# One product moved from GpSimd to VectorE, and narrowing steps spread one to a place, in a linear-attention and expert kernel

## The chip, the cores and the metric

The kernel runs on one core of one Trainium2 chip. The metric is the device time of one execution in microseconds; the value shown is the median of several runs of the same program. One more execution was taken by the hardware profiler, and every duration below comes from it.

## The reference, cut to what matters

Three parts follow one another: a gated linear recurrence over 768 time steps for 4 batches of 8 heads of width 48, a routing of the 3072 resulting tokens to 8 experts of 384 places each, and a feed-forward layer on all tokens. The change touches only the time in which the first part runs.

```python
def _attn_ref(q, k, v, f_logit):
    B, H, S, D = q.shape                      # 4, 8, 768, 48
    f = 1.0 / (1.0 + np.exp(-f_logit))
    state = np.zeros((B, H, D, D), dtype=np.float32)
    for t in range(S):
        state = f[:, :, t, :, None] * state + np.einsum('bhd,bhe->bhde', k[:, :, t], v[:, :, t])
        y[:, :, t] = np.einsum('bhd,bhde->bhe', q[:, :, t], state)
...
h = np.maximum(x[mask] @ w1[e], 0.0); out[mask] = h @ w2[e]      # expert e, its 384 tokens
...
h = x @ w_in; g = h * np.clip(h + 3.0, 0.0, 6.0) / 6.0; return (g @ w_out).astype(np.float32)
```

The weights `moe2_w_in` and `moe2_w_out` (and the experts' weights) reach the kernel as 64-bit floats; q, k, v and the decay logits are 32-bit.

## The kernel before, in words

**Units and chunks.** The recurrence is computed in chunks of 128 time steps (`C`), 24 of them (`NCH`). Two chunks make a unit of 256 steps, of which there are 12 (`NU`). Batch and time are laid end to end, so a batch is three units, and every sixth chunk starts with an empty state. Two neighbouring time steps lie in one row of 96 numbers, so a 128-row tile holds a unit, and the even step of each pair is first folded into the odd one.

**Preparing a unit.** The logits, q and k of unit u are loaded into tiles `fr`, `qr` and `kr`. `decay` (L74) makes the decay `ft` on ScalarE in two steps (L76, L77), and on VectorE the product of a pair's two decays into `pmf` (L78). `keys` (L79) writes `pmk`: on VectorE the even key times the odd step's decay (L81), on ScalarE a copy of the odd key (L82). `queries` (L83) writes `pmq` in the same way: the even query times its decay (L85), which is the product that the change moves, and a copy (L86). TensorE then transposes these tiles (L91, L112) into PSUM tiles `pT`, ScalarE copies the decays out (L94), VectorE runs running products forward (L98) and backward (L106) and scales the transposed queries and keys by them into `qt` and `kh` (L125).

**Eight slots.** That preparation of unit u is cut into slots 0 to 7 (`slot`, L129; the tables `PET` and `OPS` say which TensorE and VectorE work a slot has). While chunk j is computed, `attention` walks four of them: slots 0 to 3 while `ti` is 0, slots 4 to 7 while `ti` is 1. `tg(i)` (L277) writes one slot. In a chunk the order of the code is: slot 0 or 4; the output of the chunk before (`l_mm`, L223: TensorE L227, ScalarE copy L232, VectorE logits L229); slot 1 or 5; the scores (`ya_mm`, TensorE L145 and L151), their copy out of PSUM on ScalarE (L177) and masking on GpSimd (L178); the values (`y_mm`, TensorE L202, ScalarE copy L203); the state's products (`kv_mm`, L213), whose VectorE addition (L220, or L218 on a batch's first chunk) and GpSimd scaling (L221) wait in the list `late` for the next slot; slot 2 or 6; the decays and, for `ti` 1, the queries of the unit after; the transposed keys (`kt_mm`, L185, L186); slot 3 or 7; and for `ti` 1 the keys of the unit after.

**Narrowing.** In the same time a generator `prep` turns 64-bit weights into pairs of 32-bit numbers. For each of 12 blocks of `moe2_w_in` (`prep_in`, L928, tiles `pw` for the two words and `pm` for the result) there are three steps: A, the split of the block before (ScalarE L720 rounds `pm` into `wih`, GpSimd L721 subtracts it from `pm` into `wil`) and VectorE's shift L923; B, VectorE's L925; C, VectorE's L927 and the load of the block two further on (L933, two buffers). After them come 8 blocks of `moe2_w_out` in four steps each (`prep_out`, L947: L958 on ScalarE with L923; L963 on VectorE; L925; L927). `take` (L275) draws steps at each slot, by a table, and a second table draws some at a chunk's end:

```python
PREP=((2,0,1,0),(0,0,2,0)); END=(0,1)
...
for _ in range(PREP[ti][i] if j<20 else 2): next(prep,None)
...
if j<20:
    for _ in range(END[ti] if j>=0 else 0): next(prep,None)
```

Both tables give three steps to a chunk, so a unit carries two blocks of `moe2_w_in`. From chunk 20 on every slot takes two. A slot runs its first VectorE operation, then the steps, or the additions in `late` first where the slot has no operation of its own.

**Order.** Every engine and the SyncE queue, which issues all these loads and stores, execute in the order in which the code writes them; nothing is rearranged. After the last chunk the routing for the first expert follows, then the loading of that expert's weights and tokens, then eight experts' matrix products, which fill TensorE to the end.

Of the kernel before, what the change touches and what calls it, by code (L numbers as in the profile page):

```python
# [17 lines left out]
def attention(tc, q,k,v,f,wg, x_dram, lg, ident, pmin, ranges, prep, setup, spin):  # L18
    nc=tc.nc
    ctx=ExitStack()  # L20
    with ctx:
# [11 lines left out]
        ft=cs.tile([128,2,H,D],F32,name="ft")  # L33
# [27 lines left out]
        def load(u,nm,h0=0,h1=H):  # L61
            b,o=divmod(u*U,S)
            if nm!='v':
                src={'f':f,'k':k,'q':q}[nm]
                t=ld.tile([128,H,2*D],F32,name=nm+"r",bufs=1) if h0==0 else raw[nm,u]
                nc.sync.dma_start(t[:,h0:h1],bass.AP(tensor=src.tensor,offset=src.offset+b*H*S*D+h0*S*D+o*D,ap=[[2*D,128],[S*D,h1-h0],[1,2*D]]))
            else:
                t=VP[u%2]
                for c in range(2):
                    nc.sync.dma_start(t[:,c,:,:D],bass.AP(tensor=v.tensor,offset=v.offset+b*H*S*D+(o+c*C)*D,ap=[[D,C],[S*D,H],[1,D]]))  # L70
            raw[nm,u]=t
        view=lambda u,nm: raw[nm,u].rearrange("p h (r d) -> p r h d",d=D)
        home=lambda nm,r: perm[nm][:,r].rearrange("p a s d -> p (a s) d")[:,:,:48]
# [8 lines left out]
            else: nc.scalar.copy(home('k',1)[:,h0:h1],x[:,1])  # L82
        def queries(u,i,h0=0,h1=H):  # L83
            x=view(u,'q')[:,:,h0:h1]
            if i==0: nc.gpsimd.tensor_tensor(out=home('q',0)[:,h0:h1],in0=x[:,0],in1=ft[:,0,h0:h1],op=OP.mult)  # L85
            else: nc.scalar.copy(home('q',1)[:,h0:h1],x[:,1])  # L86
        KH={};QT={};PC={};PX={};SX={}
        V=nc.vector
# [12 lines left out]
        def kept(u):  # L101
            PC[u]=pmin[:,u]
            nc.scalar.copy(PC[u],PX[u][:,:,:,G])
# [25 lines left out]
        def slot(u,n,fill=None):  # L129

            if u<NU and n in PET: PET[n](u)
            for f,*a in OPS.get(n,()) if u<NU else ():
                f(u,*a)
                if fill: fill(); fill=None
            while late: late.pop(0)()
            if fill: fill()
# [16 lines left out]
        def ya_mm(j):  # L153

            S=s_mm(j) if 0<=j<NCH and j%6 else None
            A=a_mm(j+1) if j+1<NCH else None
            if not S or not A:
                for p in range(NP):
                    for h in range(2):
                        for s in range(2):  # L160
                            if A: A(p,s,h)
                if S:
                    for p in range(NP):
                        for s in range(2): S(p,s)
                return
            for i,p in enumerate((0,2,1,3,None,None)):
                for s in range(2):
                    if p is not None: S(p,s)
                for s in range(2):
                    if i<2 or i>3: A(i if i<2 else i-2,s,1-s)  # L170
                for s in range(2):
                    if i>1: A(i-2,s,s)
        def a_ev(j,s):
            if s==0:
                AM[j]=wk.tile([128,2,NP,C],F32,name="am")
            am=AM[j][:,s]
            nc.scalar.copy(am,pA[j][s])  # L177
            nc.gpsimd.affine_select(out=am,in_=am,pattern=[[0,NP],[1,C]],compare_op=OP.is_ge,fill=0.0,base=0,channel_multiplier=-1)  # L178
        def kt_mm(j):
            u,c=divmod(j,2)  # L180
            if j%6==5: return
            kt=wk.tile([128,4,2,64],F32,name="kt")
            pk=ps.tile([128,NP,128],F32,name="pT",bufs=PB)
            for p in range(NP):
                nc.tensor.transpose(pk[:,p],KH[u][:,p,c*C:(c+1)*C],ident)  # L185
            nc.scalar.copy(kt.rearrange("p a s d -> p a (s d)"),pk)  # L186
            KT[j]=kt
        YT={};PY={}
        def y_mm(j,part):

            u,c=divmod(j,2); first=j%6==0
            vr=raw['v',u]; last=j==NCH-1
            rows=[slice(64*s,64*s+64) for s in range(2)]
            if part==0:
                if last: PY[j]=[ps.tile([128,NP,C],F32,name=f"pA{i}") for i in range(2)]
                else: PY[j]=[ps.tile([128,NP,C],F32,name="pT",bufs=PB) for _ in range(1 if first else 2)]*(2 if first else 1)
                return
            yt=wk.tile([128,NP,C],F32,name="yt")
            for p in (0,2,1,3):
                py=PY[j][p%2]  # L200
                for s in range(2):
                    nc.tensor.matmul(py[rows[s^p%2],p],vr[:,c,2*p+s],AM[j][:,s,p],start=first,stop=first or p>1)  # L202
                if p>1 and not first: nc.scalar.copy(yt[:,p%2::2],py[:,p%2::2])  # L203
            if first: nc.scalar.copy(yt,py)
            YT[j]=yt
        def kv_mm(j):
            u,c=divmod(j,2); first=j%6==0
            if j%6==5 or j>=NCH: return
            vr=raw['v',u]
            pk=ps.tile([128,512],F32,name="pT",bufs=PB)[:,:NP*D].rearrange("p (a d) -> p a d",a=NP)  # L210
            for p in range(NP):
                for s in range(2):
                    nc.tensor.matmul(pk[64*s:64*s+64,p],KT[j][:,p,s],vr[:,c,2*p+s,:D],start=True,stop=True)  # L213
            sn=St[(j+1)%2][:,:,:D]; so=St[j%2][:,:,:D]
            def update():
                pcb=PC[u][:,:,c][:,:,None].to_broadcast([128,NP,D])
                if first:
                    nc.vector.tensor_tensor(out=sn,in0=pk,in1=pcb,op=OP.mult)  # L218
                else:
                    nc.vector.tensor_add(so,so,pk)  # L220
                    nc.gpsimd.tensor_tensor(out=sn,in0=so,in1=pcb,op=OP.mult)  # L221
            late.append(update)
        def l_mm(j):  # L223
            W=2*D+8
            px=ps.tile([128,512],F32,name="pT",bufs=PB)[:,:NP*W].rearrange("p (a e) -> p a e",a=NP)
            for p in (0,2,1,3):
                nc.tensor.matmul(px[:,p],YT[j][:,p],SW[:,p],start=True,stop=True)  # L227
            y=wk.tile([128,NP,2*D],F32,name="y")
            def logits(): nc.vector.tensor_reduce(lg[:,j],px[:,:,2*D:].rearrange("p a e -> p e a"),axis=AX.X,op=OP.add)  # L229
            if j==NCH-1: logits()  # L230
            else: late.append(logits)
            nc.scalar.copy(y,px[:,:,:2*D])  # L232
            later.append(lambda: nc.sync.dma_start(x_dram[j*C:(j+1)*C,:],y.rearrange("p a d -> p (a d)")))
# [26 lines left out]
        def refill(u,nm,i):  # L260
            if u<NU:
                {'f':decay,'k':keys,'q':queries}[nm](u,i)
                if u+1<NU and i==(0 if nm=='f' else 1): later.append(lambda: load(u+1,nm))
# [3 lines left out]
        next(prep)  # L267
        while later: later.pop(0)()
        constants,early=setup()
        PREP=((2,0,1,0),(0,0,2,0)); END=(0,1)  # L270
        for j in range(-1,NCH+1):
            tu,ti=divmod(j+1,2)
            tu+=1
            if j>=0 and j%2==0 and j//2+1<NU: load(j//2+1,'v')
            def take(i):  # L275
                for _ in range(PREP[ti][i] if j<20 else 2): next(prep,None)
            def tg(i): slot(tu,4*ti+i,(lambda: take(i)) if j>=0 else None)  # L277
            if j==NCH: spin(lambda: ps.tile([128,384],F32,name="pT",bufs=PB),TAIL[0])
            tg(0)
            if 0<=j-1<NCH: l_mm(j-1)  # L280
            if j==NCH: spin(lambda: ps.tile([128,384],F32,name="pT",bufs=PB),TAIL[1])
            tg(1)
            while later: later.pop(0)()
            if 0<=j<NCH: y_mm(j,0)
            ya_mm(j)
            if j+1<NCH:
                a_ev(j+1,0)
                a_ev(j+1,1)
            if ti==1: refill(tu+1,'f',2)
            if 0<=j<NCH: y_mm(j,1)  # L290
            if j>=0: kv_mm(j)
            tg(2)
            if ti==0 and tu<NU: kept(tu)
            if ti==0: refill(tu+1,'f',0)
            if j+1<NCH: kt_mm(j+1)
            if ti==1:
                for i in range(2): refill(tu+1,'q',i)
            tg(3)
            if ti==0: refill(tu+1,'f',1)
            if ti==1:  # L300
                for i in range(2): refill(tu+1,'k',i)
            if j>=0: next(constants,None)
            if j>=NCH-4: next(ranges,None)
            if j in (17,22,24): next(early)
            if j<20:
                for _ in range(END[ti] if j>=0 else 0): next(prep,None)
# [55 lines left out]
class Routing:  # L362
# [67 lines left out]
    def spin(s,tile,n):  # L430

        if not n: return
        t=tile()
        for _ in range(n): s.tc.nc.tensor.matmul(t[:,:128],s.ones,s.before,start=True,stop=True)
# [715 lines left out]
```

## Time and profile before

| | us |
|---|---|
| median of 3 runs (839.98 to 841.34) | 841.13 |
| the profiled execution's own time | 845.23 |
| its span, first to last instruction | 843.2 |
| TensorE busy in the span (94%) | 793.5 |
| VectorE busy (65%) | 549.6 |
| ScalarE busy (43%) | 364.0 |
| GpSimd busy (16%) | 134.7 |

The shares are averages over two very different stretches. Up to about 168 us the chunks run, with all five engines and the loads in play; from about 194 us on, the experts' products keep TensorE at work. In the trace an instruction has a start, a duration, and, in brackets, the idle time of its engine just before it with the instruction or transfer that ended it. An instruction's duration includes the time in which it has started and is held up, so the same form can show different durations.

### The profile page before, as it was taken

To read this page: it belongs to the slowest core of one execution; us is meant where nothing else is said; L and a number is where in the kernel's file an instruction comes from. 1 tells how busy PE (TensorE), PEld (TensorE's weight loads), DVE (VectorE), ACT (ScalarE), POOL (GpSimd) and SP (SyncE) were. 2 spreads that over 40 slices of the span, in tenths; PEclk is the share of its full clock that TensorE was granted. 3 is DMA by queue.
4 is the path that set the end of the run, shared out by engine and by line. 5 is a ranking of instruction groups with operands and counts; after the bars stand their busy time and mean duration, and the time that the engine had idled before them with its cause. 6 is when DMAs were issued, how large, how long until landed. Compare 5 with 4: busy or idle time off the path is not lost.

```text
span 843.2 us, 16692 instructions
## 1 busy us (share of the span) xinstructions
PE 793.5 (94%) x6387; PEld 761.9 (90%) x6387; DVE 549.6 (65%) x1522; ACT 364.0 (43%) x757; POOL 134.7 (16%) x215
## 2 busy tenths in 40 slices
PE   7887899978999999999999999999999999999994
PEld 6776788767989899899999999999999999999994
DVE  7898789777688647846875776667766523642431
ACT  4776677523244325423542454154316423541431
POOL 2665554211001100010101101100200020010001
PEclk9999899988999999999999999999999999999998
DMA  9898897272013112311422232322232321321000
GB/s 220 201 236 203 204 267 185 59 252 87 1 38 113 57 39 59 101 38 57 134 70 77 87 100 82 91 79 83 87 92 83 91 90 57 113 87 47 10 1 32
DMA packets 99032, 84.54 MB, mean 100 GB/s; under 512 B 67328, under 2 KB 86912, under 8 KB 98944
## 3 DMA queue, kind: packets, MB, share of 16 engines
q1 hardware_dynamic: 95872, 73.96, 31.5%
q0 software_dynamic: 3072, 9.44, 3.6%
q8 instruction: 52, 0.85, 0.4%
q14 instruction: 36, 0.29, 0.1%
HBM read 73.94 MB, written 9.44 MB: 99 GB/s over the span
## 4 chain that ended last, share of the span: by engine, by line
PE 57%; issue 10%; DVE 8%; ACT 2%; DMA 2%; POOL 1%; POOLq 0%; SPq 0%; DVEq 0%; ACTq 0%
PE pF L724 9%; PE acc L724 9%; PE pF L725 9%; PE pF L726 9%; PE acc L726 9%; PE acc L725 9%; DMA xg<-x_dram,q_ids 1%; DVE ga L867 1%; DVE hl L870 1%; ACT hh L869 1%; DVE w1l L773 1%; PE pF L811 1%; POOL out_dram L901 1%; DVE q_ge L502 1%; POOL xg L790 1%
## 5 line engine op out<-in xcount | busy, mean ns | idle before, releaser
L724 PE MATMUL acc<-wo,hh 128*128 128x384 f32 x384 | 134.0, 349 | 0.0
L724 PE MATMUL pF<-xh,wih 128*128 128x384 f32 x384 | 131.0, 341 | 0.0
L867 DVE SCALAR_TENSOR_TENSOR ga<-ga,pF 128x384 f32<-128x384 f32 x128 | 70.8, 553 | 92.3 <-ACT ga L866 92.0
L726 PE MATMUL acc<-wo,hh 128*128 128x384 f32 x384 | 129.7, 338 | 0.0
L725 PE MATMUL acc<-wo,hl 128*128 128x384 f32 x384 | 129.5, 337 | 0.0
L725 PE MATMUL pF<-xh,wil 128*128 128x384 f32 x384 | 129.4, 337 | 0.0
L726 PE MATMUL pF<-xl,wih 128*128 128x384 f32 x384 | 129.3, 337 | 0.0
L866 ACT ACTIVATE ga<-pF,three 128x384 f32<-128x384 f32 x128 | 74.1, 579 | 98.9 <-PE pF L726 92.1
L869 ACT CAST hh<-ga 128x384 fp32r<-128x384 f32 x128 | 65.8, 514 | 98.4 <-DVE ga L867 92.9
L870 DVE TENSOR_TENSOR hl<-ga,hh 128x384 fp32r<-128x384 f32 x128 | 71.2, 556 | 29.7 <-ACT hh L869 27.7
L832 ACT ACTIVATE hh<-pF 128x384 fp32r<-128x384 f32 x64 | 31.5, 492 | 132.4 <-PE pF L726 125.1
L901 POOL DMA_INDIRECT out_dram<-ga,q_ids x24 | 24.3, 1011 | 396.7 <-ACT ga L899 393.9
L833 DVE SCALAR_TENSOR_TENSOR hl<-pF,hh 128x384 fp32r<-128x384 f32 x64 | 35.6, 556 | 71.2 <-ACT hh L832 70.8
L724 PEld LDWEIGHTS acc<-wo,hh 128*128 128x128 f32 x384 | 72.5, 189 | 1.6 <-ACT ga L866 1.5
L725 PEld LDWEIGHTS acc<-wo,hl 128*128 128x128 f32 x384 | 72.5, 189 | 0.2 <-DVE hl L870 0.2
L726 PEld LDWEIGHTS acc<-wo,hh 128*128 128x128 f32 x384 | 72.4, 188 | 0.0
L724 PEld LDWEIGHTS pF<-xh,wih 128*128 128x128 f32 x384 | 72.2, 188 | 0.0
L725 PEld LDWEIGHTS pF<-xh,wil 128*128 128x128 f32 x384 | 72.2, 188 | 0.0
L726 PEld LDWEIGHTS pF<-xl,wih 128*128 128x128 f32 x384 | 72.1, 188 | 0.0
L724 PE MATMUL pF<-xh,w1h 128*128 128x384 f32 x192 | 66.8, 348 | 0.6 <-ACT xh L802 0.6
L724 PE MATMUL acc<-hh,w2h 128*128 128x384 f32 x192 | 65.9, 343 | 0.0
L726 PE MATMUL pF<-xl,w1h 128*128 128x384 f32 x192 | 64.9, 338 | 0.0
(285 smaller groups left out, 1623.5 us busy)
## 6 DMA issues: line engine op xcount, KB each, us to landing
wst<-in_moe_w_dram SPq DMA_DIRECT2D x58, 192.0 KB, 2.4
wst<-in_moe_w_dram SPq DMA_DIRECT2D x42, 256.0 KB, 3.0
pw<-in_moe_w_in_dram SPq DMA_DIRECT2D x12, 512.0 KB, 5.1
wo<-in_moe_w_out_dram SPq DMA_DIRECT2D x16, 384.0 KB, 4.3
pm<-in_moe_w_out_dram SPq DMA_DIRECT2D x32, 192.0 KB, 2.5
pm<-in_moe_w_in_dram SPq DMA_DIRECT2D x30, 192.0 KB, 2.6
v<-in_v_dram SPq DMA_DIRECT2D x24, 192.0 KB, 5.2
x_dram<-y SPq DMA_DIRECT2D x24, 192.0 KB, 4.9
```

Source lines behind the costliest of these rows:

```text
L502: V.scalar_tensor_tensor(ge[:,c0:c1],x[:,c0:c1,None].to_broadcast([128,c1-c0,32]),base[:,0:1],grid[:,None,:].to_broadcast([128,c1-c0,32]), ...
L724: nc.tensor.matmul(out, ahi, bhi, start=start, stop=False)
L725: nc.tensor.matmul(out, alo, bhi, start=False, stop=False)
L726: nc.tensor.matmul(out, ahi, blo, start=False, stop=stop)
L773: nc.vector.tensor_tensor(out=lo,in0=got[i],in1=hi.bitcast(F32),op=OP.subtract)
L832: nc.scalar.activation(hh,p,AF.Relu)
L833: s.defer(2,lambda: nc.vector.scalar_tensor_tensor(hl,p,0.0,hh.bitcast(F32),op0=OP.max,op1=OP.subtract))
L866: nc.scalar.activation(a,p,AF.Relu,bias=s.three[:,0:1])
L867: late(f,1,lambda: nc.vector.scalar_tensor_tensor(g,a,6.0,p,op0=OP.min,op1=OP.mult))
L869: late(f,1,lambda: nc.scalar.copy(gh,g))
L870: late(f,3,lambda: nc.vector.tensor_tensor(out=gl,in0=g,in1=gh.bitcast(F32),op=OP.subtract))
L901: st=nc.gpsimd.indirect_dma_start(out=s.out,out_offset=bass.IndirectOffsetOnAxis(ap=ids[:,t:t+1],axis=0),in_=o,in_offset=None)
```

## The change

```diff
         def queries(u,i,h0=0,h1=H):
             x=view(u,'q')[:,:,h0:h1]
-            if i==0: nc.gpsimd.tensor_tensor(out=home('q',0)[:,h0:h1],in0=x[:,0],in1=ft[:,0,h0:h1],op=OP.mult)
+            if i==0: (nc.vector if u else nc.gpsimd).tensor_tensor(out=home('q',0)[:,h0:h1],in0=x[:,0],in1=ft[:,0,h0:h1],op=OP.mult)
...
-        PREP=((2,0,1,0),(0,0,2,0)); END=(0,1)
+        PREP=((1,0,1,1),(1,0,1,1)); END=(0,0)
...
-                for _ in range(PREP[ti][i] if j<20 else 2): next(prep,None)
+                for _ in range(PREP[ti][i] if j<21 else 2): next(prep,None)
```

For units 1 to 11 the product of q and decay is issued on VectorE; the two half-width ones of unit 0 stay on GpSimd. The narrowing steps still come three to a chunk, but each alone, at the first, third and fourth slot of a chunk; none is drawn at a chunk's end; and chunk 20 takes three steps instead of eight.

The first place is VectorE in the second chunk of a unit and the start of the next (slot 6, behind L220, to slot 0); names ending in a number are buffers.

```order
+L923 TENSOR_SCALAR pm<-pw 128x512
+L85 TENSOR_TENSOR pmq<-qr,ft 128x8x48
+L125 TENSOR_TENSOR kh_126<-pT,S 128x512
+L925 SCALAR_TENSOR_TENSOR pm<-pw,pm 128x512
+L81 TENSOR_TENSOR pmk<-kr,ft 128x8x48
 L927 SCALAR_TENSOR_TENSOR pm<-pw,pm 128x512
-L923 TENSOR_SCALAR pm<-pw 128x512
-L125 TENSOR_TENSOR kh_126<-pT,S 128x512
-L81 TENSOR_TENSOR pmk<-kr,ft 128x8x48
-L925 SCALAR_TENSOR_TENSOR pm<-pw,pm 128x512
-L927 SCALAR_TENSOR_TENSOR pm<-pw,pm 128x512
-L923 TENSOR_SCALAR pm<-pw 128x512
```

Before, step C of one block and step A of the next stood together ahead of the scaled keys `kh`, with B, the next C and one more A behind the keys product; now A, the queries product and then `kh` follow one another, with B and C further on.

The second place is ScalarE from the end of a unit's preparation to the values of the next chunk (`am` masked scores, `yt` values).

```order
 L94 COPY ff_133<-pT 128x4x64
-L720 CAST wih<-pm 128x512
-L232 COPY y<-pT 128x384
-L177 COPY am<-pA_642 128x512
-L177 COPY am<-pA_643 128x512
-L203 COPY yt<-pT 128x2x128 x2
+L232 COPY y<-pT 128x384
+L177 COPY am<-pA_638 128x512
+L177 COPY am<-pA_639 128x512
+L203 COPY yt<-pT 128x2x128 x2
+L720 CAST wih<-pm 128x512
 L103 COPY pmin<-P_113 128x8
```

The rounding L720 of the first chunk of a unit stood ahead of the chunk's four copies out of PSUM; it now stands behind them, as it already did in the second chunk. With it GpSimd's subtraction L721 moves behind the masking L178 and, in that chunk, ahead of the state's scaling L221. On the SyncE queue the loads of `pw`, of which two stood together ahead of the load of `qr`, stand apart, one of them now ahead of the load of `fr`.

## Rows read from the trace of the kernel before

**Rows 1.** The page of the kernel before: its span.

```profile
span 843.2 us, 16692 instructions
```

**Rows 2.** Stretches: length, busy us (TensorE, loads, VectorE, ScalarE, GpSimd), clock, DMA share, GB/s.

```profile
20.00:40.00 20.00, 18.63 (x341) 16.46 (x332) 17.82 (x32) 14.72 (x32) 12.04 (x20) 1.00 1.00 224
40.00:60.00 20.00, 15.34 (x262) 13.46 (x258) 17.72 (x35) 13.94 (x32) 12.49 (x20) 1.00 0.81 215
60.00:80.00 20.00, 16.20 (x292) 14.86 (x294) 17.75 (x31) 13.12 (x30) 11.61 (x16) 1.00 0.96 228
80.00:100.00 20.00, 16.78 (x244) 14.76 (x236) 15.28 (x27) 10.06 (x24) 10.65 (x18) 0.83 0.72 176
100.00:120.00 20.00, 17.04 (x295) 15.66 (x296) 16.04 (x39) 14.76 (x34) 10.58 (x14) 1.00 0.94 249
...
140.00:160.00 20.00, 17.84 (x313) 15.45 (x309) 19.53 (x47) 10.91 (x27) 5.86 (x11) 1.00 0.35 99
```

**Rows 3.** VectorE's timeline: first and seventh full-width keys product (start, us).

```profile
24.83 1.37 DVE L81 TENSOR_TENSOR pmk<-kr,ft 128x384 f32<-128x384 f32 x1
...
107.83 0.54 DVE L81 TENSOR_TENSOR pmk<-kr,ft 128x384 f32<-128x384 f32 x1
```

**Rows 4.** Waits of 20 to 108 us: total us, times, longest.

```profile
ACT wih L720 <- DVE pm L927: 19.1, 12, 2.6
...
DVE St L220 <- PE pT L213: 7.5, 4, 4.1
```

**Rows 5.** The same wait, 20 to 190 us.

```profile
DVE St L220 <- PE pT L213: 12.2, 8, 4.1
```

**Rows 6.** All engines' timeline, 52 to 67 us (start, us, engine, line).

```profile
51.20 1.25 DVE L81 TENSOR_TENSOR pmk<-kr,ft 128x384 f32<-128x384 f32 x1
...
51.99 1.32 POOL L85 TENSOR_TENSOR pmq<-qr,ft 128x384 f32<-128x384 f32 x1
...
52.37 1.50 DVE L925 SCALAR_TENSOR_TENSOR pm<-pw,pm 128x512 uint32<-128x512 uint32 x1
...
53.90 0.69 DVE L927 SCALAR_TENSOR_TENSOR pm<-pw,pm 128x512 uint32<-128x512 uint32 x1
...
54.63 0.62 ACT L720 CAST wih<-pm 128x512 fp32r<-128x512 f32 x1 [2.58 <-DVE pm L927]
...
55.24 0.43 DVE L923 TENSOR_SCALAR pm<-pw 128x512 uint32<-128x512 uint32 x1 [0.65 <-DMA pw<-in_moe_w_in_dram]
...
56.92 0.66 PE L112 MATMUL pT<-ident,pmk 128*128 128x128 f32 x4 [2.46 <-ACT yt L203]
...
61.13 0.55 DVE L78 TENSOR_TENSOR pmf<-ft 128x384 f32<-128x384 f32 x1
...
62.97 0.68 DVE L125 TENSOR_TENSOR kh<-pT,S 128x512 f32<-128x512 f32 x1
...
63.66 0.33 PE L151 MATMUL pT<-qt,St 64*64 64x128 f32 x2
```

**Rows 7.** VectorE's groups by line, 20 to 250 us (count, busy us, mean ns, idle before).

```profile
L925 DVE SCALAR_TENSOR_TENSOR pm<-pw,pm 128x512 uint32<-128x512 uint32 x12 | 12.7, 1054 | 0.0
L81 DVE TENSOR_TENSOR pmk<-kr,ft 128x384 f32<-128x384 f32 x10 | 10.6, 1055 | 0.0
...
L923 DVE TENSOR_SCALAR pm<-pw 128x512 uint32<-128x512 uint32 x12 | 7.4, 617 | 2.1 <-DMA pw<-in_moe_w_in_dram 2.1
```

**Rows 8.** GpSimd's groups by line, 20 to 250 us.

```profile
L721 POOL TENSOR_TENSOR wil<-pm,wih 128x512 fp32r<-128x512 f32 x12 | 15.7, 1308 | 13.6 <-ACT wih L720 13.6
L85 POOL TENSOR_TENSOR pmq<-qr,ft 128x384 f32<-128x384 f32 x10 | 12.1, 1207 | 0.0
```

**Rows 9.** A stretch of 4 us at the lower clock, columns as in rows 2.

```profile
88.00:92.00 4.00, 4.00 (x60) 3.48 (x61) 1.00 (x3) 1.33 (x3) 0.20 (x1) 0.50 1.21 234
```

**Rows 10.** VectorE's timeline, 149 to 166 us: eight narrowing steps (first, last).

```profile
149.92 0.55 DVE L963 TENSOR_TENSOR wo<-pm,wo 128x384 fp32r<-128x384 f32 x1
...
156.10 0.35 DVE L923 TENSOR_SCALAR pm<-wo 128x384 uint32<-128x384 uint32 x1
```

## The prediction

> **What bounds the kernel now.** I read the views in this order: busy time by stretches, to find where the change lies; the waits and the timeline there, to find what ends last; then the groups by line, for durations. The span is 843.2 us [rows 1], the profiled execution took 845.23, and the runs have a median of 841.13. I make the sum as a difference in the profiled execution and take it off the median, which assumes that the 4.1 us between the two do not lie in what changes.
>
> The change lies in the first 168 us. There VectorE is the fullest engine but for TensorE: 17.8 of 20 us in the stretch from 20, as much in the two after it, 19.5 from 140 [rows 2]. What it does not fill is waiting. From one keys product to the next is one unit of two chunks, and six units, in which `moe2_w_in` is narrowed, take 107.83 - 24.83 = 83.0 us, 13.8 each [rows 3].
>
> Two kinds of loss are to be seen. First, GpSimd holds VectorE up. The queries product runs on GpSimd from 51.99 to 53.31; VectorE's L925 starts at 52.37 and ends at 53.87, 0.56 behind it [rows 6]. It was not slowed, it stood still until GpSimd was done. The keys product ahead of it takes 1.25 [rows 6], beside GpSimd's subtraction L721, where it has 0.54 at its best [rows 3]. The scaling of `kh`, with an input from PSUM, shows 0.68 [rows 6] and I take it as not held. Second, there is a ring of waits. ScalarE reaches its rounding L720 and waits 2.58 us for VectorE's L927, that is for step C; the copies that stand behind L720 on ScalarE come late, TensorE idles 2.46 us for `yt` [rows 6], and some us later VectorE idles for TensorE's state products. From 20 to 108 us ScalarE waits 19.1 us so, 12 times, and VectorE 7.5, 4 times [rows 4].
>
> **The change, part by part.** *The queries product.* GpSimd loses ten products of 1.21 us [rows 8] and an eleventh in the setup, which I cost at nothing, since the loads of unit 1 set the pace there. On VectorE the nearest row is the decay product, the same 128x384 form, at 0.55 [rows 6]; the upper bound is a held operation, 1.50 as L925 shows [rows 6]. I take 0.55, since GpSimd has less to do beside it, and count the holding apart. In the six units that is +3.3 us.
>
> *What VectorE is held for.* L925 has a mean of 1.054 over 12 [rows 7]; five of them, one in a unit, lie at 1.49 to 1.50 like the row above, so the others have (12.7 - 7.5)/7 = 0.74, and the queries product costs VectorE 5 x 0.76 = 3.8. The keys products lose 10.6 - 10 x 0.54 = 5.2 [rows 3, 7], most of it to L721. Step A, 7.4 us in 12 [rows 7], has 0.43 when alone [rows 6] and loses 7.4 - 12 x 0.43 = 2.2. Together 11.2, some 1.9 a unit. The 12 subtractions of 1.31 us [rows 8] stay, and in a unit's second chunk one now falls beside the queries product or L925. I leave VectorE held for one whole subtraction a unit, 1.3, and win 0.6 x 6 = 3.6. With the +3.3 VectorE's own work comes out level, -0.3. The ends are -7.9 (all 11.2 won) and +5.2 (each product held to 1.50, 6 x 1.5 = 9.0, less the 3.8).
>
> *One step to a place.* Step C now comes a slot or two ahead of step A, so L720 finds its input ready; in a unit's first chunk it also moves behind four copies. ScalarE's 19.1 us should shrink to a few. In itself that wins nothing, ScalarE having room (14.7 of 20 us at its fullest [rows 2]); what counts is VectorE's idle time. Of its 7.5 us I take 6 back, since TensorE gets its 2.4 us a unit again. The bounds are 0, if TensorE, busy for up to 18.6 of 20 us [rows 2], is late anyway, and 7.5. The loads of `pw` are now drawn in single steps with more time between each and its step A, so VectorE's three waits for them, 2.1 us [rows 7], go; on the queue they stand ahead of the loads of `fr` and `qr`, which have about a unit to land, and the buffer they fill is free, so nothing is held behind them. Bounds: -2.1 and 0.
>
> *Moved on the queues.* GpSimd's scaling of the state, L221, now follows L721 in a unit's first chunk. The next chunk's L151 needs it; ahead of that TensorE has five to six groups of transposes and products, so I cost it at nothing. Without that cover it would cost up to a subtraction, 1.3 a unit. The load of `qr` waits for VectorE instead of GpSimd and has a unit to land: nothing.
>
> *Chunk 20.* Eight steps lie there between 149.92 and 156.45, of 0.55 to 0.35 [rows 10], while VectorE is 98% full [rows 2], six of them ahead of the unit's last `kh`. Five go to the two chunks behind, where VectorE has idle time: from 108 us on it waits 12.2 - 7.5 = 4.7 us for L213 [rows 4, 5]. I take -1.5, between 0 and 5 x 0.45 = -2.3.
>
> *Units after 108 us.* L721 is gone there, and of five products, 2.8 us, most falls into those 4.7: +0.3, between 0 and +2.8.
>
> Sum: -0.3 - 6 - 2.1 - 1.5 + 0.3 = -9.6. What follows, routing, weights and experts, hangs on the last chunk's logits and moves by all of it. I round to -9: 836.2 profiled, **832.0 us** as median.
>
> The Trainium skill (SBUF — State Buffer, Who interferes with whom) says that a VectorE instruction with two SBUF inputs and a GpSimd one that reads SBUF exclude each other for their whole length, whichever starts first. L925's 1.50 agrees [rows 6]. By that rule alone an unlucky queries product lasts 0.55 + 1.31 us, and the sum would be worse by 6 x 1.31 = 7.9, close to no change.
>
> **The rivals.** *VectorE is too full (slower).* The moved product stands ahead of `kh`, and TensorE takes up `kh` without a gap: it ends at 63.65, the next chunk's first products start at 63.66 [rows 6]. If the product is held to 1.50 in all eleven units and only one L927 of 0.69 [rows 6] leaves that place, `kh` is late by 0.8 each time, 8.8 us; the ring's 6 us stay lost, with TensorE late for `kh` instead; against it stand only 3.8 from L925 and 2.1 from the loads. That is +2.9: 844.0. It decides from 0.69 + 5.9/11 = 1.23 us a product. For it: the keys product is held to 1.25 in that place now. Against it: GpSimd has less to do there, and L721 starts only behind L221. The Trainium skill (Perfetto Trace Analysis, Optimizing Scalar/DVE Operations) advises taking work off a saturated VectorE, to ScalarE or even GpSimd, which speaks against this change; it adds that between those two it might not help.
>
> *The transfers bind.* In the four stretches from 20 to 100 us the DMA engines' share is 1.00, 0.81, 0.96 and 0.72, with 224, 215, 228 and 176 GB/s, 211 on average [rows 2]. If 224 is the most that these loads reach, a unit takes at least 13.8 x 211/224 = 13.0 us, and the six win 4.9 instead of 8.4; with the rest about -6: 835. Against it: 249 GB/s from 100 to 120 [rows 2], and VectorE's 2.1 us are the only large wait for a load.
>
> *The clock.* From 88 to 92 us TensorE ran at 0.50 of its clock, 1.2 GHz [rows 9], after one of its 2 us waits. VectorE's longest wait, 4.1, lies there; the other three have (7.5 - 4.1)/3 = 1.1 [rows 4], so the drop costs 3.0, which my 6 hold. If it comes in three units instead, -9 + 9 leaves no change, 841. Against it: TensorE's waits become fewer.
>
> **How the numbers follow.** A measurement of this kernel tells 0.2%, 1.7 us, from no change. Chances: the forecast 0.68 (826 to 837); transfers 0.12; the clock's worse form, or terms that cancel, 0.08; VectorE too full 0.12. The first two are faster: 0.80; same 0.08; slower 0.12. The range is 825 to 840.5. Its low end is the sum with the better bound of the held time, -9.6 - 7.6 = -17.2, not quite reached; its high end leaves out the slower rival and most of no change.
>
> **What would show it.** Right: the six units from keys product to keys product in 75 us or less instead of 83; L85 on VectorE near 0.55 and L925 near 0.7; L720's waits for L927 a few us in all; TensorE's 2 us waits for `yt` gone; no wait of VectorE for `pw`; the routing 8 to 10 us earlier. Wrong: L85 at 1.2 or more, TensorE waiting for `kh`, or VectorE idle for L213 as before. If the chunks end earlier and the time stays, something behind them bounds.

## The result, and the profile after

The changed kernel takes 830.47 us (median of 4 runs, 828.00 to 833.07) against 841.24 for the kernel before (4 runs, 839.98 to 843.36): a ratio of 0.987, 95% interval 0.9834 to 0.9906, or 10.8 us faster. Its profiled execution took 830.40 us, with a span of 828.7.

From the page of the changed kernel, the span and the busy time of each engine:

```profile
span 828.7 us, 16684 instructions
PE 790.8 (95%) x6387; PEld 760.5 (92%) x6387; DVE 551.0 (66%) x1533; ACT 364.6 (44%) x757; POOL 122.8 (15%) x204
```

VectorE (DVE) is as busy as before (549.6 us then), GpSimd (POOL) 11.9 us less. What went is idle time, in the stretches in which the change lies. Changed kernel, stretches of 20 us, columns as in [rows 2]:

```profile
20.00:40.00 20.00, 19.70 (x372) 17.74 (x370) 19.49 (x38) 16.27 (x36) 10.86 (x20) 1.00 1.00 227
40.00:60.00 20.00, 17.87 (x289) 15.42 (x285) 19.86 (x40) 15.34 (x34) 14.04 (x22) 1.00 1.03 251
60.00:80.00 20.00, 19.27 (x336) 17.30 (x334) 19.46 (x41) 15.82 (x36) 11.69 (x19) 1.00 0.95 257
80.00:100.00 20.00, 17.56 (x315) 15.34 (x314) 17.76 (x35) 13.71 (x31) 10.05 (x13) 1.00 1.06 269
```

VectorE fills 97 to 99% of the first three; before it was 89% [rows 2]. The loads run at 227 to 269 GB/s where they had at most 228 there, so 228 was not the most that they reach.

The keys product, the mark of [rows 3], moved within its chunk. A mark that stayed is the decay product L78; I take unit 2's and unit 8's. Six units so marked, kernel before (same columns):

```profile
22.88:105.14 82.26, 68.36 (x1134) 61.16 (x1134) 71.49 (x132) 54.49 (x123) 49.54 (x74) 0.96 0.87 211
```

And the changed kernel:

```profile
23.22:95.10 71.88, 66.99 (x1156) 59.43 (x1154) 70.62 (x139) 56.07 (x125) 45.19 (x71) 1.00 1.00 247
```

They take 10.4 us less. VectorE's busy time falls by 0.9, though it has six products of q and decay more; its idle time falls from 82.26 - 71.49 = 10.8 to 1.3 us. From unit 8's L78 to the last, three units on, it takes 1.1 less, from there to the routing's last maximum (L474) 2.65 less, and unit 2's L78 starts 0.34 later: L474 comes at 155.45 instead of 169.21, 13.8 us earlier.

The waits of the changed kernel from 20 to 108 us (columns as in [rows 4]), the same two as there:

```profile
DVE St L220 <- PE pT L213: 0.8, 2, 0.4
ACT wih L720 <- DVE pm L927: 0.7, 1, 0.7
```

They were 7.5 and 19.1 us [rows 4]. No wait of VectorE for `pw` is left, nor one of TensorE's products for `yt` above 0.2 us. VectorE's groups of the changed kernel from 20 to 250 us, columns as in [rows 7]:

```profile
L925 DVE SCALAR_TENSOR_TENSOR pm<-pw,pm 128x512 uint32<-128x512 uint32 x12 | 10.2, 850 | 0.0
...
L923 DVE TENSOR_SCALAR pm<-pw 128x512 uint32<-128x512 uint32 x12 | 7.9, 658 | 0.0
L85 DVE TENSOR_TENSOR pmq<-qr,ft 128x384 f32<-128x384 f32 x10 | 7.8, 777 | 0.0
...
L78 DVE TENSOR_TENSOR pmf<-ft 128x384 f32<-128x384 f32 x10 | 7.7, 769 | 0.4 <-ACT ft L77 0.4
```

The moved product (L85) takes 0.777, not 0.55; L925 fell from 1.054 to 0.850; the keys product L81 from 1.055 to 0.546. The decay product L78, which had 0.55 [rows 6], now is held. One unit on VectorE:

```profile
46.12 0.88 DVE L78 TENSOR_TENSOR pmf<-ft 128x384 f32<-128x384 f32 x1
46.92 0.34 DVE L220 TENSOR_TENSOR St<-St,pT 128x192 f32<-128x192 f32 x1
47.19 0.59 DVE L923 TENSOR_SCALAR pm<-pw 128x512 uint32<-128x512 uint32 x1
47.69 0.86 DVE L85 TENSOR_TENSOR pmq<-qr,ft 128x384 f32<-128x384 f32 x1
48.47 0.68 DVE L125 TENSOR_TENSOR kh<-pT,S 128x512 f32<-128x512 f32 x1
49.07 1.17 DVE L925 SCALAR_TENSOR_TENSOR pm<-pw,pm 128x512 uint32<-128x512 uint32 x1
50.16 0.55 DVE L81 TENSOR_TENSOR pmk<-kr,ft 128x384 f32<-128x384 f32 x1
50.63 0.68 DVE L927 SCALAR_TENSOR_TENSOR pm<-pw,pm 128x512 uint32<-128x512 uint32 x1
```

No instruction here is preceded by idle time, and the three products stand at 0.88, 0.86 and 0.55: the holding is spread, not gone.

### The profile page after: what moved, and what is told of

Its sections match the earlier page's. It is cut to its first block, busy times and chain, and to the rows that moved or that the text cites. A ratio compares the mean times of both kernels' runs of the same rounds, so it can differ in the third digit from the quotient of the medians.

```text
span 828.7 us, 16684 instructions
## 1 busy us (share of the span) xinstructions
PE 790.8 (95%) x6387; PEld 760.5 (92%) x6387; DVE 551.0 (66%) x1533; ACT 364.6 (44%) x757; POOL 122.8 (15%) x204
## 4 chain that ended last, share of the span: by engine, by line
PE 57%; issue 10%; DVE 9%; ACT 2%; DMA 1%; POOL 1%; POOLq 0%; SPq 0%; DVEq 0%; ACTq 0%
PE pF L724 9%; PE acc L724 9%; PE pF L725 9%; PE pF L726 9%; PE acc L726 9%; PE acc L725 9%; DVE ga L867 2%; DVE hl L870 1%; ACT hh L869 1%; DVE w1l L773 1%; ACT ga L866 1%; PE pF L811 1%; POOL out_dram L901 1%; DMA xg<-x_dram,q_ids 1%; DVE q_ge L502 1%
## 5 line engine op out<-in xcount | busy, mean ns | idle before, releaser
L725 PE MATMUL pF<-xh,w1l 128*128 128x384 f32 x192 | 65.3, 340 | 0.0
```

The source lines that it names most:

```text
L725: nc.tensor.matmul(out, alo, bhi, start=False, stop=False)
```

## The experiments

Each ratio is to the kernel before on the same chip in the same session, with its 95% interval (medians before: 842.23 in the first four, 841.67 in the next four, 843.22 in the last four).

**The two halves apart.** The change has two parts, so each was run by itself. First the product alone:

```diff
-            if i==0: nc.gpsimd.tensor_tensor(out=home('q',0)[:,h0:h1],in0=x[:,0],in1=ft[:,0,h0:h1],op=OP.mult)
+            if i==0: (nc.vector if u else nc.gpsimd).tensor_tensor(out=home('q',0)[:,h0:h1],in0=x[:,0],in1=ft[:,0,h0:h1],op=OP.mult)
```

> Only the queries product goes to VectorE; narrowing steps as before. Theory (the ring of waits through ScalarE's rounding L720 carries most of the gain, the product little): 838 to 843 us, L720 still waits some 15 to 20 us for L927 between 20 and 108 us, VectorE still idles 6 us or more for L213, while L925 falls from 1.05 to about 0.75. Rival (GpSimd holding VectorE up is the main loss): 834 or less, and the six units shrink from 83 to below 78 us.

Measured: 839.39 us, ratio 0.9964 (0.9948 to 0.9979). L85 takes 0.607 (mean of the seven from 20 to 108 us) and L925 falls to 0.719; VectorE's busy time in the six units falls by 3.0, to 68.50. All the waits of [rows 4] stay in smaller form (L720 15.3, L220 5.0). The product alone wins 0.36%.

Then the order of the steps alone:

```diff
-        PREP=((2,0,1,0),(0,0,2,0)); END=(0,1)
+        PREP=((1,0,1,1),(1,0,1,1)); END=(0,0)
...
-                for _ in range(PREP[ti][i] if j<20 else 2): next(prep,None)
+                for _ in range(PREP[ti][i] if j<21 else 2): next(prep,None)
```

> Only the narrowing steps are spread and chunk 20 gets three; the queries product stays on GpSimd. Theory (the ring): 831 to 835 us, L720's waits below 3 us, VectorE's waits for L213 below 2 us before 108 us, the six units 72 to 75 us. Rival (GpSimd's holding is the main loss): 837 or more.

Measured: 834.22 us, ratio 0.9902 (0.9881 to 0.9923). Idle time of VectorE in the six units 1.65 us instead of 10.8, but busy time up by 3.4, since GpSimd's products hold it (L925 1.08, L927 0.87); so the units take 76.53 us, where 72 to 75 were expected. The order wins 0.98%; the two parts add up to the 1.3% of both.

**Is ScalarE's wait the cause?** The prediction has a ring that begins with ScalarE waiting for step C at L720. In the kernel before, the split (L720, L721) was issued with step B of the next block instead of step A:

```diff
-                split()
...
-                yield from join(m,got[i])
+                parts=join(m,got[i]); next(parts)
+                yield
+                split()
+                next(parts)
+                yield
+                next(parts,None)
```

> The kernel before with one edit: the split of a block (ScalarE L720, GpSimd L721) is issued with step B of the next block instead of step A, so VectorE's order, the tables and the queries product are all as before, and only the wait of ScalarE for step C goes. Theory (the ring alone, through ScalarE's order, makes TensorE and then VectorE idle): L720's waits fall from 19 us to below 4, TensorE's 2 us waits for yt go, 833 to 837 us. Rival (the places of the steps on VectorE are what counts, two in one place delaying kh): 839 to 842.

Measured: 843.82 us, ratio 1.0011 (0.9992 to 1.0031). Waits of this kernel from 20 to 108 us:

```profile
ACT pmin L103 <- DVE P L98: 9.6, 6, 3.2
...
DVE St L220 <- PE pT L213: 6.4, 4, 3.2
...
ACT wih L720 <- DVE pm L927: 4.5, 4, 1.7
PE pT L227 <- ACT kt L186: 3.9, 3, 1.5
...
PE pT L112 <- DVE lg L229: 3.0, 3, 2.4
PE pT L227 <- DVE lg L229: 2.9, 2, 1.8
```

ScalarE's wait at L720 fell by 14.6 us and TensorE's waits for `yt` went, and nothing was won. Part of ScalarE's waiting came back at L103, for VectorE's scan L98 (9.6 us, before 1.3). TensorE now waits for VectorE directly, at the logits' reduction L229, and VectorE's wait at L220 is there as before. The first link of the ring, L720's wait, was not needed for the loss.

**The kernel before a second time**, unchanged, for how much one profile of it tells:

> The kernel before, unchanged, profiled a second time, to see whether TensorE's drop to half its clock near 88 us is in every execution. If the drop made the 4 us between the profiled 845.2 and the median 841.2: a span near 839 without a drop in that stretch, and the unit there at about 13.7 us instead of 16.8. If it is always there: the same drop, a span near 843 or the difference elsewhere.

Measured: 838.92 us, span 836.9, 6.3 less than the profile that the prediction was made from. Its stretch at the place of [rows 9], and the one ahead of it:

```profile
84.00:88.00 4.00, 1.82 (x15) 1.57 (x15) 3.93 (x11) 4.00 (x10) 3.34 (x4) 1.00 0.81 225
88.00:92.00 4.00, 4.00 (x90) 3.67 (x90) 2.42 (x6) 2.58 (x6) 2.08 (x7) 1.00 1.27 254
```

The clock stays at 1.00 there. It fell at two other places of the six units, so the mean over them is 0.96 in both profiles:

```profile
44.00:46.00 2.00, 2.00 (x11) 2.00 (x11) 1.93 (x5) 1.92 (x3) 1.67 (x5) 0.50 1.08 299
71.00:74.00 3.00, 2.81 (x13) 2.41 (x13) 2.93 (x8) 1.68 (x5) 0.98 (x2) 0.50 1.13 309
```

The longest L220 wait is 1.9 us instead of 4.1, and L474 comes at 166.59, 2.6 us earlier; the other 3.7 us lie behind the chunks. L720's waits are 18.6 us as before.

**Chunk 20.** In the changed kernel, chunk 20 drew its eight steps again:

```diff
-                for _ in range(PREP[ti][i] if j<21 else 2): next(prep,None)
+                for _ in range(PREP[ti][i] if j<20 else 2): next(prep,None)
```

> The changed kernel with chunk 20 taking eight narrowing steps again (the limit 20 instead of 21). My term: 0.7 to 2 us slower than the changed kernel, 831 to 833 against its 830.5, with the stretch from the last decay product to the routing's last maximum at about 26.5 us instead of 25.1. Rival (the chunks' end is bound elsewhere): within 0.5 us of it.

Measured: 832.48 us, ratio 0.9894 (0.9865 to 0.9922), against 0.987. The times alone don't separate the two; the trace does: from the last L78 to L474 it is 156.84 - 129.59 = 27.25 us, in the changed kernel 25.07, in the one before 27.72. The six units are the same (71.86). That is 2.2 us; but from unit 8's L78 to the last, where both kernels have the same code, this profile is 0.8 us shorter (34.52 against 35.28), and L474 comes only 1.4 later. So chunk 20's steps are worth some 1.4 to 2.2 us.

**ScalarE's wait put back.** In the changed kernel the split stands right behind step C, so that L720 waits again while VectorE's order stays:

```diff
-                split()
...
-                split=lambda i=i,m=m,c=c: split_raw(nc,m,wih[:,i//4,c],wil[:,i//4,c],nc.gpsimd)
+                split_raw(nc,m,wih[:,i//4,c],wil[:,i//4,c],nc.gpsimd)
...
-            split()
```

> The changed kernel with VectorE's order unchanged, but the split of a block (L720 on ScalarE, L721 on GpSimd) issued straight behind its step C, so that L720 stands ahead of the copies again and waits for an L927 issued just before it. Theory one (ScalarE's wait by itself makes the loss): L720 waits 10 us or more for L927, TensorE idles for yt again, 835 or more. Theory two (after the split-later run: the loss came from two steps of VectorE ahead of the scans at a chunk's start, and ScalarE's wait only showed VectorE's lateness): L720 waits some us, and the time stays within 2 us of 830.5.

Measured: 831.39 us, ratio 0.9868 (0.9837 to 0.9899). Waits from 20 to 108 us:

```profile
ACT wih L720 <- DVE pm L927: 17.7, 12, 2.5
...
PE pT L112 <- ACT yt L203: 1.0, 4, 0.4
...
DVE St L220 <- PE pT L213: 0.7, 1, 0.7
```

ScalarE waits as long as in the kernel before, and the time is that of the changed kernel. With the run of the later split, the wait was neither needed for the loss nor enough for it.

**One pair taken apart in the kernel before.** Only step A moves, from slot 0 to slot 2 of a unit's first chunk:

```diff
-        PREP=((2,0,1,0),(0,0,2,0)); END=(0,1)
+        PREP=((1,0,2,0),(0,0,2,0)); END=(0,1)
```

> The kernel before with one number of the table changed: in a unit's first chunk step A goes from slot 0, behind step C, to slot 2, so it stands behind the scans L98 on VectorE, and L720 behind the copies on ScalarE; the second chunk keeps C and A together and the queries product stays on GpSimd. Theory two (VectorE's order at the chunk's start): 836 to 838, more than half of the steps' 8 us, since in the profile the large TensorE waits all come at that chunk's start; the waits for pw go as well. Theory one would say the same of ScalarE's wait there; against both, a result of 840 or more means that the second chunk's pair of steps counts as much.

Measured: 842.31 us, ratio 1.0001 (0.9982 to 1.0021). The waits for `pw` are gone, L720's fell to 10.6, L220's to 4.0 us, and nothing was won: TensorE waits 3.5 and 3.2 us for L229, and VectorE is held for longer (busy 76.23 us in the six units, before 71.49), which uses up most of the idle time that went.

**The subtraction moved too.** In the changed kernel L721 runs on VectorE:

```diff
-                split=lambda i=i,m=m,c=c: split_raw(nc,m,wih[:,i//4,c],wil[:,i//4,c],nc.gpsimd)
+                split=lambda i=i,m=m,c=c: split_raw(nc,m,wih[:,i//4,c],wil[:,i//4,c],nc.vector)
```

> The changed kernel with the subtraction of the split (L721) on VectorE as well, 12 of about 0.69 us instead of 12 of 1.42 on GpSimd. If GpSimd's subtraction is what holds VectorE in the changed kernel (9 to 10 us over L78, L85, L923 and L925), those go to their free 0.55, 0.55, 0.40 and 0.68, VectorE wins about 8 and pays 8.3: 829 to 832. If the masking L178 and the state's scaling L221 hold it: 834 to 838.

Measured: 831.25 us, ratio 0.9886 (0.9856 to 0.9917). The twelve subtractions cost VectorE 8.8 us; L925 falls to 0.678 and L923 to 0.498, and the busy time rises by 2.1. What GpSimd no longer holds pays for most of it: no gain.

**What fits these.** VectorE and TensorE hand work to each other at two places of a unit: at the state's update behind L78 (L218 or L220) VectorE needs TensorE's L213, and at the first L229 of the next unit VectorE releases a PSUM tile that TensorE needs. In the kernel before, five of a unit's six steps stand from the first place to the second (L927, L923, L925, L927, L923) and one in the other stretch; the run with the later split has five, the one with step A moved four, the changed kernel three. From the start of L218 or L220 to the start of that L229 VectorE takes 6.93 us a unit in the kernel before and 4.95 in the changed one; the rest of the unit takes 6.84 and 7.14, though it now has two steps more (means of the six units). With the later split it is 7.06 and 6.61, with step A moved 6.44 and 7.11. In the full stretch TensorE waits for VectorE, through `yt` or L229, whichever comes first; in the empty one VectorE waits for TensorE. The last four runs test this against the other reading, that single steps instead of pairs are what counts, and test that VectorE sets the pace.

*Pairs, but three and three*, in the changed kernel:

```diff
-        PREP=((1,0,1,1),(1,0,1,1)); END=(0,0)
+        PREP=((0,0,2,0),(0,0,2,0)); END=(1,1)
```

> The change with steps A and C again in one place each (two calls of A and two of C between the stages, two of B at the chunk's end), but so that each of the two stretches between the two places where TensorE and VectorE hand over holds three steps. ScalarE's wait at the narrowing comes back. By the theory that what counts is how many of a unit's six steps lie in each stretch, three and three is all that is needed: 830 to 834 us, with VectorE's wait for TensorE at L220 under 2 us between 20 and 108 us. By the theory that what counts is one step to a place, as in the changed kernel, the pairs cost again: 837 us or more, about what the change of the product alone gives (839.4).

Measured: 832.89 us, ratio 0.9862 (0.9836 to 0.9887). Waits from 20 to 108 us:

```profile
ACT wih L720 <- DVE pm L927: 12.3, 12, 1.6
...
DVE St L220 <- PE pT L213: 5.4, 5, 1.3
...
PE pT L227 <- ACT kt L186: 4.3, 3, 1.6
```

*Single steps, but five and one*, in the changed kernel:

```diff
-        PREP=((1,0,1,1),(1,0,1,1)); END=(0,0)
+        PREP=((1,1,1,0),(0,0,1,1)); END=(0,1)
```

> The change with one step to a place, never two in a row, but five of a unit's six steps in the stretch from a chunk's last stages to the next chunk's first and one in the other, as the kernel before has them. By the theory of three and three: 836 to 840 us, with VectorE waiting for TensorE at L220 again (4 us or more between 20 and 108 us) and TensorE for VectorE in the crowded stretch. By the theory that one step to a place is what counts: 830 to 833 us, and L220 under 2 us.

Measured: 837.60 us, ratio 0.9923 (0.9899 to 0.9948). Waits from 20 to 108 us:

```profile
ACT wih L720 <- DVE pm L927: 11.6, 8, 2.1
...
DVE St L220 <- PE pT L213: 5.8, 4, 2.2
PE pT L185 <- ACT yt L203: 5.3, 3, 1.8
...
PE pT L112 <- ACT yt L203: 3.4, 2, 1.7
```

Both times are those of three and three. The line of L220 was forecast wrong for the pairs: 5.4 us instead of under 2. L720 waits 12 us in both; TensorE's 8.7 us for `yt` at L185 and L112 are only in the second.

Two things stay open. In the second run B is directly followed by C on VectorE, so it is not free of pairs; the first has two pairs a unit and is the faster all the same. And in all these kernels with five and one, three of a unit's steps stand between the keys product L81 and that first L229, with four and two it is two, with three and three one. That these alone count, and not the whole stretch, is a rival that no run separates.

*The decay product twice* (L78, the product of a pair's two decays, which the expectations call that of k and decay), first in the changed kernel, then in the one before:

```diff
-            else: nc.vector.tensor_mul(perm['f'].rearrange("p a s d -> p (a s) d")[:,h0:h1,:48],ft[:,0,h0:h1],ft[:,1,h0:h1])
+            else:
+                for _ in range(2 if u else 1): nc.vector.tensor_mul(perm['f'].rearrange("p a s d -> p (a s) d")[:,h0:h1,:48],ft[:,0,h0:h1],ft[:,1,h0:h1])
```

> The changed kernel with the product of k and decay (L78) issued a second time on VectorE, into the same tile, for 11 of the units. It was measured at 569 ns in the kernel before, 769 with what it is held in the changed one, so 6 to 8 us of VectorE's time. If VectorE sets the pace of the chunks now: 6 us or more slower than the changed kernel, 836 to 839 us. If transfers or TensorE do: at most 1.5 us slower, 830 to 832 us.

Measured: 838.31 us, ratio 0.9940 (0.9917 to 0.9963): (0.9940 - 0.9872) x 841 = 5.7 us slower than the changed kernel, give or take 3.6 by the two intervals.

> The kernel before with the same second product of k and decay for 11 of the units. It stands right ahead of the place where VectorE waits for TensorE (L220, 12.2 us in twelve waits). By the theory that VectorE's waits there are empty time, part of the 6 us hides in them: 1 to 3 us slower than before, and L220's waits get shorter by the rest. If VectorE's work is on the path at that place all the same: 6 us slower, 847 us or more, and L220's waits stay.

Measured: 843.24 us, ratio 0.9999 (0.9979 to 1.0019). The same work costs nothing there. Its wait at that place from 20 to 108 us (every line number behind L78 is one higher in this kernel):

```profile
DVE St L221 <- PE pT L214: 2.5, 4, 1.0
```

The wait had 7.5 us [rows 4], and 6.0 in the second profile (the 12.2 us to 190 us are in eight waits [rows 5], not twelve). In the six units VectorE is busy for 74.79 us and idle for 3.9. So there was room in which even more work than forecast is free; the changed kernel has no such room. One thing blurs this: in the profile of the doubled product the clock is 1.00 over the six units (78.73 us long), where both profiles of the kernel before have 0.96.

The six units, from L78 to L78, in one table; idle is the length less VectorE's busy time, the next column TensorE's waits at L112 and L185 for `yt` or L229 in that time, the last its mean granted clock:

| kernel | steps | length | VectorE busy | idle | TensorE waits | clock |
|---|---|---|---|---|---|---|
| before | 5 + 1 | 82.26 | 71.49 | 10.8 | 11.9 | 0.96 |
| before, again | 5 + 1 | 80.33 | 70.83 | 9.5 | 11.7 | 0.96 |
| before, split later | 5 + 1 | 81.70 | 72.73 | 9.0 | 3.0 | 0.94 |
| product alone | 5 + 1 | 78.06 | 68.50 | 9.6 | 8.4 | 0.98 |
| changed, five and one | 5 + 1 | 77.13 | 69.65 | 7.5 | 8.7 | 0.98 |
| before, step A moved | 4 + 2 | 81.30 | 76.23 | 5.1 | 6.7 | 0.98 |
| steps alone | 3 + 3 | 76.53 | 74.88 | 1.7 | 3.0 | 1.00 |
| changed, pairs | 3 + 3 | 72.49 | 67.50 | 5.0 | 0 | 1.00 |
| changed, split with C | 3 + 3 | 72.06 | 70.17 | 1.9 | 1.0 | 1.00 |
| changed, subtraction on VectorE | 3 + 3 | 73.82 | 72.74 | 1.1 | 0 | 1.00 |
| changed | 3 + 3 | 71.88 | 70.62 | 1.3 | 0.2 | 1.00 |

With five and one these waits are 8.4 to 11.9 us, but for the later split, where 2.9 of TensorE's waiting stand at L227 instead; with three and three they are at most 3.0, and that only where GpSimd's products still hold VectorE. The share doesn't settle VectorE's idle time alone: with pairs 5.0 us stay, and are nearly made good by 3.1 us less busy time. Why VectorE is held less there was not tried. Four and two has half the idle time of the kernel before and no gain, since its busy time is the longest of all.

The clock goes with the share in the table: in every profile with five and one or four and two it falls below 1.00 in the six units, with three and three in none. The kernels with the decay product twice are the other way round, 0.98 in the changed one and 1.00 in the one before. The unit in which most of the fall of [rows 9] lies takes 105.14 - 88.97 = 16.17 us, in the second profile, where the clock held there, 13.67. So a part of what the even share wins may be TensorE's clock; how much, no run separates.

## Why the prediction was right, point by point

The time (832.0 forecast, 832.1 by its own sum, and 830.47 measured) and the sign were right, and the sum of -9.6 stands against -10.8 in the medians. One mechanism behind the sum was named wrongly.

- *The queries product.* Right. Alone it wins 0.36%, and with the new order the six units' busy time falls by 0.9 (from the second profile of the kernel before by 0.2) where -0.3 was forecast. The parts of that were off and made up for each other: L85 is held to 0.777 on average instead of 0.55, L925 is at 0.850 instead of near 0.7, and L78 is held now, while L81 lost all its holding. The rule of the Trainium skill (SBUF — State Buffer, Who interferes with whom), by which the sum would have been worse by 7.9, is borne out in single instructions (L925 ends 0.55 behind a subtraction, last section) but not in what it was feared to cost: L85 lost 0.23 us each, not 1.31. The advice of the Trainium skill (Perfetto Trace Analysis, Optimizing Scalar/DVE Operations) to take work off a saturated VectorE, even to GpSimd, would have gone the wrong way here; its warning that between those two it might not help agrees with those 0.36%.
- *"One step to a place", -6.* The size was right, VectorE's idle time at L220 fell by 6.7 us (by 5.2 from the second profile), but the step from ScalarE's L720 to it failed; that the size came out all the same is in part luck. That wait can be taken away without a gain (843.82) and put back without a loss (831.39). What the runs show in its place is the share of steps between the two handovers: five and one loses, three and three doesn't, with pairs or without. Whether the whole stretch counts or only its end, and how much of it is the clock, stays open. ScalarE's wait was one way by which a late VectorE reached TensorE.
- *The loads of `pw`, -2.1.* Those waits are gone, as forecast. But with step A moved they were gone too, without a gain, so that this was a term of its own is not shown.
- *Chunk 20, -1.5.* Some -1.4 to -2.2, inside the bounds.
- *Units after 108 us, +0.3.* Not shown either way: from unit 8's L78 to the last it is -1.1 against the first profile of the kernel before and -0.15 against the second, and two profiles of the same code there differ by 0.8.
- *The 4.1 us between profile and median.* Taken not to lie in what changes; of the 6.3 us between the two profiles of the kernel before, 2.6 lie ahead of L474. From the second profile, L474 moves by 166.59 - 155.45 = 11.1 us, close to the 10.8 of the medians; from the first by 13.8. Both are more than the 8 to 10 that were named as a sign.
- *The rivals.* VectorE too full: it is full now, as the doubled product shows, but L85's 0.777 stays below the 1.23 us from which that rival decides. Transfers: 247 GB/s over the six units, above the 224 that were taken as their most. The clock: 1.00 in all four stretches to 100 us. The 3.0 us that the prediction's 6 hold for its fall are 2.2 by the second profile, whose longest wait at L220 is 1.9 instead of 4.1, but that profile has falls at other places.

## What to carry to other kernels

When two engines hand work to each other at two places of a loop, count how much filler work stands in each stretch between them, and try to even it out before going after any single wait: here a wait that was removed without that came back at another place. A wait that is long in the list need not cost anything; putting it back in the faster version is as good a test as taking it out of the slower one. An engine at 89% can have free time in one stretch and be late in the other, and only added work (here nothing in the one version, 5.7 us in the other) tells which.

## What was not expected of the hardware

The fall of the clock has no fixed place in a program. From 88 to 92 us the kernel before had a granted clock of 0.50, 1.2 GHz, in one profile [rows 9], and 1.00, 2.4 GHz, in the other, which had 0.50 at two other places. TensorE's wait just ahead does not tell the two apart. In the first profile TensorE idled 2.10 us, worked from 84.68 on, and the clock fell in the microsecond from 86:

```profile
84.68 0.66 PE L185 MATMUL pT<-ident,kh 128*128 128x128 f32 x4 [2.10 <-ACT yt L203]
...
85.00:86.00 1.00, 1.00 (x12) 0.97 (x9) 0.96 (x4) 1.00 (x3) 0.98 (x2) 1.00 1.01 331
86.00:87.00 1.00, 0.93 (x5) 0.72 (x4) 1.00 (x2) 1.00 (x2) 0.80 (x3) 0.54 1.21 305
```

In the second it idled 2.11 us at the same place of the code, and the clock stayed up:

```profile
86.12 0.66 PE L185 MATMUL pT<-ident,kh 128*128 128x128 f32 x4 [2.11 <-ACT yt L203]
...
87.00:88.00 1.00, 0.93 (x8) 0.69 (x7) 1.00 (x4) 1.00 (x3) 0.86 (x2) 1.00 1.15 319
```

What decided between the two was not found.

GpSimd's masking L178, which has one input, holds a VectorE product of two SBUF inputs as the subtraction does. GpSimd's rows of the changed kernel beside the unit shown above:

```profile
45.95 1.54 POOL L178 TENSOR_SCALAR_AFFINE_SELECT am<-am 128x512 f32<-128x512 f32 x2 [2.16 <-ACT am L177]
47.46 0.67 POOL L221 TENSOR_TENSOR St<-St,pmin 128x192 f32<-128x192 f32 x1
48.10 1.59 POOL L721 TENSOR_TENSOR wil<-pm,wih 128x512 fp32r<-128x512 f32 x1
```

The decay product takes 0.88 beside L178, while the state's update behind it, with an input from PSUM, has its usual 0.34. The queries product ends 0.42 us behind L221 (48.55 against 48.13), so it went ahead of L721, which had its input and then shows 1.59 where 1.31 is its mean before [rows 8]; L925 ends 0.55 behind L721 (50.24 against 49.69). No run takes L178 away, but with the subtraction on VectorE nothing of GpSimd's but L178 lies beside the decay product, and it is held all the same (GpSimd's row, then VectorE's):

```profile
34.82 1.23 POOL L178 TENSOR_SCALAR_AFFINE_SELECT am<-am 128x512 f32<-128x512 f32 x2 [1.69 <-ACT am L177]
...
35.45 1.00 DVE L78 TENSOR_TENSOR pmf<-ft 128x384 f32<-128x384 f32 x1
```

Of the six decay products of that run, the four that start while an L178 is under way take 0.89 to 1.00 us, the other two 0.56 and 0.55.
